# Sparse attention and two feed-forward stages: chunks of 4, 3, 5 and 4 blocks, and decoding tied behind the activations on VectorE

## The chip, the cores and the metric

The program runs on one core of a Trainium2 chip. The metric is the device time of one execution in microseconds (us). The engines are TensorE (PE, with its weight loads PEld), VectorE (DVE), ScalarE (ACT), GpSimd (POOL) and SyncE (SP, which starts the DMAs here). "L414" is line 414 of the kernel before; the changed kernel has one line more from line 473 on and three more at its end, so L486, L489 and L511 of before are L487, L490 and L512 after it.

## What is computed

```python
x = attention(q, k, v)              # 2 x 8 heads x 768 x 64: a window of +-15 keys and 24 block summaries
h = x @ w_in                        # 1536 x 512 by 512 x 2048
x = (h - np.tanh(h)) @ w_out        # 2048 x 512
rms = np.sqrt(np.mean(x * x, axis=-1, keepdims=True) + 1e-06)
xn = x / rms * rms_g
g = xn @ w_gate                     # 512 x 1536
silu = g * (1.0 / (1.0 + np.exp(-g)))
out = (silu * (xn @ w_val)) @ w_out2
```

The weights are 64-bit floats, which the kernel turns into pairs of 32-bit values on the chip.

## The kernel before

**Decoding.** A weight block of 512 x 128 (or 128 x 512) comes as 128 x 1024 32-bit words by one DMA (`load`). `words` makes 32-bit floats of it: ACT scales one half (L162), and three DVE operations put sign, exponent and mantissa together (L163, L164, L165). `split` makes a high part (ACT, L170) and a low part (POOL, L173), since every product is three matmuls: high by high, low by high, high by low (L395 to L397, L401 to L403). The decoding of one block is a Python generator, `one`, cut into portions at its `yield`s; for the second feed-forward `pair_of` also forms sums of quarters on POOL (L207 to L218), as Strassen's scheme with seven products needs them. `work()` emits the next portion; `adv(dt)` moves a planned clock on and emits a portion each `DEC` microseconds of it. A block needs a slot of ten (later thirteen) buffers, which is free again when the last group of tokens has used it.

**First feed-forward.** The 1536 tokens are four groups of 384, the 2048 inner columns sixteen blocks of 128, in chunks (`NCH`). The loops run over chunk, group, block; one pass of the inner body is a **step**, 64 in all. `up_step` does twelve matmuls into one of two PSUM banks `h`, then the activation: ACT's tanh (L413), DVE's difference (L414, which frees the bank), ACT's high part (L416), DVE's low part (L417). `down_step`, three steps later (`LAG`), does nine matmuls into three accumulators `acc`; at the last block of a chunk DVE adds these to `part` (L437; for the first chunk a copy, L435). Twelve steps lie among the attention, the other 52 behind it.

**Between the two.** After a group's last step, `norm` takes the mean square on ACT (L447), twelve small DVE operations that form the inverse root (L448 to L454), and a diagonal matrix from ACT (L457). `turn` transposes and scales `part` with matmuls (L474), ACT copies them out (L476), and `operand` forms the operands (DVE L486, ACT L488, DVE L489). `prepare` puts them on the planned clock.

**Second feed-forward.** Twelve units (six column blocks, two halves of the tokens) of fourteen products each (`unit2`, `product`); the activated pairs end with DVE's L511. Twelve down products (`down2`) of the unit before are filled in. The value weights' second half is read first by the unit's product "6" into `accx`.

**Order.** Tile, the layer underneath, takes the instructions with their dependences in the order of the Python text and lays each engine's order out by a simulated timeline. Each engine then works strictly in that order. `SLOTS_A`, `DEC`, the planned times and the text's order are the means of steering. `tc.issue_after(ins)` puts the instructions of its block that run on `ins`'s engine behind `ins` in that engine's order, without a semaphore.

Of the kernel before, what the change touches and what calls it, by code (L numbers as in the profile page):

```python
# [25 lines left out]
KT = TPB // 2  # L26
LOC = 64 + 2 * WIN
WID = LOC + NB
NCH = [4, 4, 4, 4]
NG = NT // GW  # L30
NP = FF2 // 256
SLOTS_A = 10
# [16 lines left out]
DTR = 6  # L49
DPV = 10  # L50
DVL = 10
DEC = (2.3, 1.9)
TP0 = 1.2
TP1 = 1.0
TC = 0.6
# [32 lines left out]
def attn_moe_kernel(ctx: ExitStack, tc: tile.TileContext, ins, out, dbg=None):  # L88
# [24 lines left out]
    def f(ap):  # L113
        return ap.bitcast(F32)
# [272 lines left out]
    for j, nch in enumerate(NCH):  # L387
# [1 line left out]
            for m in range(m0, m0 + nch):  # L389
                steps.append((j, g, m, m == m0, m == m0 + nch - 1))  # L390
        m0 += nch
    acc, part, gs = {}, {}, {}

    def triple(o, wh, wl, xh, xl, start, stop, **kw):
        T.matmul(o, wh, xh, start=start, stop=False, **kw)  # L395
        T.matmul(o, wl, xh, start=False, stop=False, **kw)  # L396
        T.matmul(o, wh, xl, start=False, stop=stop, **kw)  # L397

    def down(o, w, g, j, first, last):
        js = slice(j * 128, (j + 1) * 128)  # L400
        T.matmul(o, g[:, 0, js], w[:, 0], start=first, stop=False)  # L401
        T.matmul(o, g[:, 1, js], w[:, 0], start=False, stop=False)  # L402
        T.matmul(o, g[:, 0, js], w[:, 1], start=False, stop=last)  # L403

    def up_step(i):
        _, g, m, _, _ = steps[i]
        h = ps_h.tile([128, 512], F32, name="h")[:, 0:GW]
        w, x = wt["w_in", m], xT[g]
        for kk in range(KD):
            ws = slice(kk * 128, (kk + 1) * 128)  # L410
            triple(h, w[:, 0, ws], w[:, 1, ws], x[:, :, 0, kk], x[:, :, 1, kk], kk == 0, kk == KD - 1)
        t = tmp()
        A.activation(t, h, AF.Tanh)  # L413
        V.tensor_tensor(t, h, t, ALU.subtract)  # L414
        gg = gs[i] = gp.tile([128, 2, GW], F32R, name="g")
        A.activation(gg[:, 0], t, AF.Copy)  # L416
        V.tensor_tensor(gg[:, 1], t, f(gg[:, 0]), ALU.subtract)  # L417

    def down_step(i):
        j, g, m, first, last = steps[i]  # L420
        gg = gs.pop(i)
        for t in range(g * GT, g * GT + GT):
            if first:
                acc[t] = ps_a.tile([128, 512], F32, name="acc")
            down(acc[t], wt["w_out", m], gg, t - g * GT, first, last)
            if last:
                evac(acc.pop(t), t, j == 0)

    def evac(a, t, first):
# [40 lines left out]
    def turn(tp, kk, kh, half):  # L470
        g, k4 = 2 * tp + half, 2 * kh + kk
        ps = state["ps_t"].tile([128, 512], F32, name="t2")
        for j in range(GT):
            T.matmul(ps[:, j * 128:(j + 1) * 128], part[g * GT + j][:, k4 * 128:(k4 + 1) * 128], dg[g][:, j * 128:(j + 1) * 128], start=True, stop=True)  # L474
        xs[tp, kk, kh, half] = tmp()
        A.activation(xs[tp, kk, kh, half], ps[:, 0:GW], AF.Copy, scale=rg[:, k4:k4 + 1])  # L476
        adv(0.33)
# [23 lines left out]
    def unit2(p, tp, fill):  # L501
# [5 lines left out]
        def pair(s, row, half):  # L507
            g[row, half] = gp.tile([128, 2, GW], F32R, name="g")
            hi, lo = g[row, half][:, 0], g[row, half][:, 1]
            A.activation(hi, s, AF.Copy)  # L510
            V.tensor_tensor(lo, s, f(hi), ALU.subtract)  # L511

        product(ga, wg, tp, 1, True)
        s11 = tmp()
# [113 lines left out]
    n0 = NCH[0] * (NG - 1)  # L628
    at = TM0
    for i in range(n0):  # L630
        _, g, m, first, last = steps[i]
        req = [f"pv{g * GT + GT - 1}", f"w{m}"]
        if i >= LAG:
            req.append(f"dn{i - LAG}")
        task(f"up{i}", at, lambda i=i: up_step(i), *req)
        at += DM0
        task(f"dn{i}", at + LAG * DM0, lambda i=i: down_step(i), f"up{i}", f"w{NCH[0] + m}")
# [11 lines left out]
    def work():  # L649
        if free["gen"] is None:  # L650
            if nxt["job"] >= len(jobs):
                return False
            free["gen"] = decode(*jobs[nxt["job"]])
            nxt["job"] += 1
        r = next(free["gen"], 0)
        if r == 0:
            free["gen"] = None
        return r != "blocked"

    def adv(dt):  # L660
        free["t"] += dt
        if inside:
            return
        inside.append(1)
        while later and later[0][0] <= free["t"]:
            heapq.heappop(later)[2]()
        while free["at"] <= free["t"]:
            free["at"] = free["at"] + DEC[1 if prev else 0] if work() else free["t"] + 0.1
        inside.pop()

    def need(*keys):
# [5 lines left out]
    def prepare(tp, half, t, dt):  # L677
        if half == 0:
            operand_tiles(tp)
        for kk in range(2):  # L680
            for kh in range(2):
                at(t, lambda kk=kk, kh=kh: turn(tp, kk, kh, half))
                t += 0.5
            for n in (5, 6, 7, 4, 3) if half else (1, 2):
                at(t, lambda kk=kk, n=n: operand(tp, kk, n))
                t += dt
# [3 lines left out]
    for i in range(n0, len(steps) + LAG):  # L690
        if i < len(steps):
# [14 lines left out]
            if steps[i][1] == NG - 1 and ("w_in", steps[i][2]) not in LENT:  # L706
                free["n"] += 1
            adv(2.1)
        j, g, m, first, last = steps[i - LAG]
        need(("w_out", m))  # L710
        down_step(i - LAG)
        if g == NG - 1 and ("w_out", m) not in LENT:
            free["n"] += 1
        adv(2.1)
        if j == len(NCH) - 1 and last:
            t = free["t"]
            norm(g)
            prepare(g // 2, g % 2, t + 6.5, (1.0, 1.3, 1.0, 1.1)[g])

    for p in range(NP):  # L720
        need(("w_gate", p))
# [94 lines left out]
```

## Time and profile before

| | us |
|---|---|
| median of 3 runs | 673.13 (672.78 to 675.08) |
| profiled execution | 676.15 |
| its span, first to last instruction | 674.4 |
| PE busy in the span | 628.4 (93%) |
| DVE, ACT, POOL busy | 467.2, 324.4, 234.8 |

The span falls into attention with the first twelve steps (0 to about 125), the other 52 steps (to about 386), and the second feed-forward. The profiled execution lies 3.0 us above the median. A wait is put down to the engine whose semaphore came last; busy time of PE is modelled at its ends.

### The profile page before, as it was taken

The page shows a single profiled execution, that of the slowest core. Times are in us where ns is not written, and L with a number is a line of the kernel's source. Part 1 is how long each engine was busy: PE and PEld are TensorE (multiplying, and loading weights), DVE is VectorE, ACT ScalarE, POOL GpSimd, SP SyncE. Part 2 cuts the span into 40 slices and gives each one's busy share as a digit, 9 for nine tenths or more (in the row PEclk, how much of TensorE's full clock was granted, in tenths as well). Part 3 has the DMA queues.
Part 4 walks back from the last instruction along what each step waited for, and adds up shares of the span by engine and source line. Part 5 has one row for each costly group of instructions (what it writes and reads, how often), then busy time and mean ns, then how long its engine had stood idle before and what let it go on. Part 6 is the DMA issues. An engine that isn't in the chain of part 4 may idle for free.

```text
span 674.4 us, 9837 instructions
## 1 busy us (share of the span) xinstructions
PE 628.4 (93%) x3576; PEld 568.0 (84%) x3576; DVE 467.2 (69%) x979; ACT 324.4 (48%) x783; POOL 234.8 (35%) x237
## 2 busy tenths in 40 slices
PE   3769999989889879999999879999999999999997
PEld 3669898878777769999999779989999999999995
DVE  5899655499999873334448768777958968765545
ACT  2865676555455342223457666445444345353230
POOL 1568612034344730003003123527645556372100
PEclk9888999999999989999999989999999999999999
DMA  9995421144443330000000200211301402100013
GB/s 329 342 288 182 144 81 48 64 156 142 139 156 130 125 110 12 1 0 32 1 0 33 64 0 32 95 62 41 132 16 63 126 1 93 64 1 0 1 57 130
DMA packets 19641, 58.92 MB, mean 87 GB/s; under 512 B 2168, under 2 KB 5496, under 8 KB 19592
## 3 DMA queue, kind: packets, MB, share of 16 engines
q1 hardware_dynamic: 19592, 58.29, 25.7%
q8 instruction: 28, 0.46, 0.3%
q14 instruction: 21, 0.17, 0.1%
HBM read 54.84 MB, written 3.15 MB: 86 GB/s over the span
## 4 chain that ended last, share of the span: by engine, by line
PE 52%; DVE 15%; DMA 7%; issue 3%; ACT 3%; POOL 1%; DVEq 0%; SPq 0%; ACTq 0%
PE t L401 4%; PE h L395 4%; PE t L402 4%; PE t L403 4%; PE h L397 4%; PE h L396 4%; PE acc L395 4%; PE acc L396 4%; PE acc L397 3%; DVE dt L164 3%; DVE dt L165 3%; PE acc L403 3%; PE acc L402 3%; DMA raw<-w_out 3%; PE acc L401 3%
## 5 line engine op out<-in xcount | busy, mean ns | idle before, releaser
L173 POOL TENSOR_TENSOR w<-dt,w 128x512 fp32r<-128x512 f32 (+1 forms) x59 | 76.7, 1303 | 123.4 <-ACT w L170 109.0
L395 PE MATMUL h<-x,w 128*128 128x384 f32 x264 | 91.4, 346 | 6.2 <-DVE s L414 5.2
L397 PE MATMUL h<-x,w 128*128 128x384 f32 x264 | 89.8, 342 | 3.8 <-DVE x L382 3.8
L396 PE MATMUL h<-x,w 128*128 128x384 f32 x264 | 89.6, 339 | 0.0
L162 ACT ACTIVATE da<-raw 128x512 f32<-128x512 f32 x68 | 45.6, 671 | 88.3 <-DMA raw<-w_out 38.0
L173 POOL TENSOR_TENSOR w<-sf,w 128x256 fp32r<-128x256 f32 (+1 forms) x36 | 39.5, 1101 | 103.0 <-ACT w L170 101.7
L414 DVE TENSOR_TENSOR s<-h,s 128x384 f32<-128x384 f32 x64 | 35.3, 552 | 53.5 <-ACT s L413 53.5
L165 DVE SCALAR_TENSOR_TENSOR dt<-raw,dt 128x512 uint32<-128x512 uint32 x68 | 63.1, 930 | 0.7
L437 DVE TENSOR_TENSOR part<-t,part 128x512 f32<-128x512 f32 x60 | 40.3, 685 | 30.3 <-PE t L403 30.3
L395 PEld LDWEIGHTS h<-x,w 128*128 128x128 f32 x264 | 50.0, 190 | 12.1 <-DVE s L414 8.4
L164 DVE SCALAR_TENSOR_TENSOR dt<-da,dt 128x512 uint32<-128x512 uint32 x68 | 57.8, 852 | 3.2 <-ACT da L162 1.3
L402 PE MATMUL t<-w,g 128*128 128x512 f32 x144 | 56.9, 395 | 0.6 <-DVE g L511 0.6
L395 PE MATMUL acc<-x,w 128*128 128x384 f32 x168 | 56.9, 339 | 0.2 <-DVE part L437 0.2
L163 DVE TENSOR_SCALAR dt<-raw 128x512 uint32<-128x512 uint32 x68 | 42.7, 629 | 20.4 <-POOL w L173 6.1
L403 PE MATMUL t<-w,g 128*128 128x512 f32 x144 | 56.7, 394 | 0.0
L396 PE MATMUL acc<-x,w 128*128 128x384 f32 x168 | 56.5, 336 | 0.0
L397 PE MATMUL acc<-x,w 128*128 128x384 f32 x168 | 56.4, 337 | 0.0
L401 PE MATMUL t<-w,g 128*128 128x512 f32 x144 | 54.9, 394 | 0.3 <-DVE part L437 0.3
L397 PEld LDWEIGHTS h<-x,w 128*128 128x128 f32 x264 | 50.1, 190 | 5.1 <-DVE x L382 4.3
L413 ACT ACTIVATE s<-h 128x384 f32<-128x384 f32 x64 | 30.9, 483 | 48.8 <-PE h L397 48.6
L401 PE MATMUL acc<-w,g 128*128 128x512 f32 x132 | 51.0, 400 | 3.4 <-DVE part L437 3.2
L402 PE MATMUL acc<-w,g 128*128 128x512 f32 x132 | 52.1, 394 | 0.0
(130 smaller groups left out, 1548.5 us busy)
## 6 DMA issues: line engine op xcount, KB each, us to landing
raw<-w_out SPq DMA_DIRECT2D x28, 512.0 KB, 3.3
raw<-w_in SPq DMA_DIRECT2D x16, 512.0 KB, 3.7
q<-q SPq DMA_DIRECT2D x12, 512.0 KB, 7.8
raw<-w_gate SPq DMA_DIRECT2D x12, 512.0 KB, 3.4
raw<-w_val SPq DMA_DIRECT2D x12, 512.0 KB, 3.4
kw<-kw SPq DMA_DIRECT2D x8, 576.0 KB, 6.9
v<-vw SPq DMA_DIRECT2D x12, 384.0 KB, 5.3
out_dram<-part SPq DMA_DIRECT2D x12, 256.0 KB, 2.0
```

The source lines that it names most:

```text
L162: A.activation(a, r[:, :, 1].bitcast(F32), AF.Copy, scale=2.0 ** -112)
L163: V.tensor_scalar(t, r[:, :, 0], 29, None, ALU.logical_shift_right)
L164: V.scalar_tensor_tensor(t, a.bitcast(U32), 3, t, ALU.logical_shift_left, ALU.bitwise_or)
L165: V.scalar_tensor_tensor(t, r[:, :, 1], 0x80000000, t, ALU.bitwise_and, ALU.bitwise_or)
L173: G.tensor_tensor(lo, d, f(hi), ALU.subtract)
L395: T.matmul(o, wh, xh, start=start, stop=False, **kw)
L396: T.matmul(o, wl, xh, start=False, stop=False, **kw)
L397: T.matmul(o, wh, xl, start=False, stop=stop, **kw)
L401: T.matmul(o, g[:, 0, js], w[:, 0], start=first, stop=False)
L402: T.matmul(o, g[:, 1, js], w[:, 0], start=False, stop=False)
L403: T.matmul(o, g[:, 0, js], w[:, 1], start=False, stop=last)
L437: V.tensor_tensor(part[t], a, part[t], ALU.add)
```

## The change

The chunks become 4, 3, 5 and 4 blocks. Portions that `adv` emits are put, on DVE, behind the last low part traced so far (L417 or L511), and the turning products, on PE, behind the last product traced so far. The planned distance of portions in the first feed-forward is 1.8 in place of 2.3, and a group's turning is planned 9 in place of 6.5 behind its last step. `need` still emits portions without a tie.

```diff
-NCH = [4, 4, 4, 4]
+NCH = [4, 3, 5, 4]
-DEC = (2.3, 1.9)
+DEC = (1.8, 1.9)
...
-        T.matmul(o, wh, xl, start=False, stop=stop, **kw)
+        last["PE"] = T.matmul(o, wh, xl, start=False, stop=stop, **kw)
...
-        T.matmul(o, g[:, 0, js], w[:, 1], start=False, stop=last)
+        last["PE"] = T.matmul(o, g[:, 0, js], w[:, 1], start=False, stop=end)
...
-        V.tensor_tensor(gg[:, 1], t, f(gg[:, 0]), ALU.subtract)
+        last["DVE"] = V.tensor_tensor(gg[:, 1], t, f(gg[:, 0]), ALU.subtract)
...
-        for j in range(GT):
-            T.matmul(ps[:, j * 128:(j + 1) * 128], part[g * GT + j][:, k4 * 128:(k4 + 1) * 128], dg[g][:, j * 128:(j + 1) * 128], start=True, stop=True)
+        with tc.issue_after(last["PE"].ins):
+            for j in range(GT):
+                T.matmul(ps[:, j * 128:(j + 1) * 128], part[g * GT + j][:, k4 * 128:(k4 + 1) * 128], dg[g][:, j * 128:(j + 1) * 128], start=True, stop=True)
...
-            V.tensor_tensor(lo, s, f(hi), ALU.subtract)
+            last["DVE"] = V.tensor_tensor(lo, s, f(hi), ALU.subtract)
...
-            free["at"] = free["at"] + DEC[1 if prev else 0] if work() else free["t"] + 0.1
+            with tc.issue_after(last["DVE"].ins):
+                done = work()
+            free["at"] = free["at"] + DEC[1 if prev else 0] if done else free["t"] + 0.1
...
-            prepare(g // 2, g % 2, t + 6.5, (1.0, 1.3, 1.0, 1.1)[g])
+            prepare(g // 2, g % 2, t + 9, (1.0, 1.3, 1.0, 1.1)[g])
```

The order up to the last attention steps is the same. DVE's order differs from its 343rd row on, and PE's from its 349th.

**DVE, from the L414 of one step to the next, in the second chunk.** Before, from step 17 to step 18:

```order
L414 TENSOR_TENSOR s<-h,s 128x384
L165 SCALAR_TENSOR_TENSOR dt<-raw,dt 128x512
L163 TENSOR_SCALAR dt<-raw 128x512
L417 TENSOR_TENSOR g<-s,g 128x384
L164 SCALAR_TENSOR_TENSOR dt<-da,dt 128x512
L435 COPY part_1858<-acc 128x512
L165 SCALAR_TENSOR_TENSOR dt<-raw,dt 128x512
L163 TENSOR_SCALAR dt<-raw 128x512
L164 SCALAR_TENSOR_TENSOR dt<-da,dt 128x512
L435 COPY part_1868<-acc 128x512
L165 SCALAR_TENSOR_TENSOR dt<-raw,dt 128x512
L414 TENSOR_TENSOR s<-h,s 128x384
```

After the change, from step 22 by way of step 23 to step 24:

```order
L414 TENSOR_TENSOR s<-h,s 128x384
L165 SCALAR_TENSOR_TENSOR dt<-raw,dt 128x512
L417 TENSOR_TENSOR g<-s,g 128x384
L163 TENSOR_SCALAR dt<-raw 128x512
L164 SCALAR_TENSOR_TENSOR dt<-da,dt 128x512
L165 SCALAR_TENSOR_TENSOR dt<-raw,dt 128x512
L414 TENSOR_TENSOR s<-h,s 128x384
L417 TENSOR_TENSOR g<-s,g 128x384
L163 TENSOR_SCALAR dt<-raw 128x512
L164 SCALAR_TENSOR_TENSOR dt<-da,dt 128x512
L165 SCALAR_TENSOR_TENSOR dt<-raw,dt 128x512
L414 TENSOR_TENSOR s<-h,s 128x384
```

Before, two whole decodings and the end of a third lie between one step's L414 and the next, parts of them between L414 and L417; after the change one does at most, behind that step's L417. In the whole order before, the 31 decodings from the ninth to the 39th stand between the L414s of steps 11 and 36, and the next behind step 50's. After the change the 28 from the ninth to the 36th stand between the L414s of steps 12 and 48, with 23 of the operations L435 and L437 among them.

**PE, end of the first feed-forward.** `g_3583` and `g_3666` are the activations of steps 62 and 63, `part2_1712` (`part2_1715` after the change) belongs to the third group, `h_3839` is a product of the second feed-forward in the bank that step 63's L414 frees. Before, the end of step 62's down product and the third group's first turning:

```order
L403 MATMUL acc_3692<-x2_2789,g_3583 128x512
L474 MATMUL t2_3719<-s_3649,part2_1712 128x128
L474 MATMUL t2_3725<-s_3649,part2_1712 128x128
L474 MATMUL t2_3719<-s_3649,part2_1717 128x128
L474 MATMUL t2_3725<-s_3649,part2_1717 128x128
L474 MATMUL t2_3719<-s_3649,part2_1722 128x128
L474 MATMUL t2_3725<-s_3649,part2_1722 128x128
L395 MATMUL h_3839<-x2_3220,w_3263 128x384
L396 MATMUL h_3839<-x2_3220,w_3263 128x384
L397 MATMUL h_3839<-x2_3220,w_3263 128x384
L395 MATMUL h_3839<-x2_3220,w_3263 128x384
L396 MATMUL h_3839<-x2_3220,w_3263 128x384
```

After the change, from the last matmul of the same product into `h_3839`, over step 63's down product:

```order
L397 MATMUL h_3839<-x2_3260,w_3054 128x384
L401 MATMUL acc_3682<-w_2783,g_3666 128x512
L401 MATMUL acc_3686<-w_2783,g_3666 128x512
L401 MATMUL acc_3690<-w_2783,g_3666 128x512
L402 MATMUL acc_3682<-w_2783,g_3666 128x512
L403 MATMUL acc_3682<-w_2783,g_3666 128x512
L402 MATMUL acc_3686<-w_2783,g_3666 128x512
L403 MATMUL acc_3686<-w_2783,g_3666 128x512
L402 MATMUL acc_3690<-w_2783,g_3666 128x512
L403 MATMUL acc_3690<-w_2783,g_3666 128x512
L475 MATMUL t2_3732<-s_3643,part2_1715 128x128
L475 MATMUL t2_3732<-s_3643,part2_1720 128x128
```

The third group's turnings have moved from ahead of step 63's down product to behind it, and the second half of the second group's from ahead of step 59's down product to behind it.

**DVE, second feed-forward.** `dt_4592` is the second half of the third value block. Before, it begins behind the sixth of the 48 L511s:

```order
L511 TENSOR_TENSOR g_4145<-s_4063,g_4145 128x384
L435 COPY part_4035<-t2_4028 128x512
L557 TENSOR_TENSOR s_4124<-accx_4040,s_4124 128x384
L163 TENSOR_SCALAR dt_4592<-raw_4517 128x512
L511 TENSOR_TENSOR g_4161<-s_4124,g_4161 128x384
L164 SCALAR_TENSOR_TENSOR dt_4592<-da_4591,dt_4592 128x512
L163 TENSOR_SCALAR dt_4704<-raw_4685 128x512
L511 TENSOR_TENSOR g_4172<-s_4071,g_4172 128x384
L165 SCALAR_TENSOR_TENSOR dt_4592<-raw_4517,dt_4592 128x512
```

After the change it begins behind the fourteenth (L512 there):

```order
L512 TENSOR_TENSOR g_4580<-s_4450,g_4580 128x384
L163 TENSOR_SCALAR dt_4592<-raw_4517 128x512
L518 TENSOR_TENSOR s_4646<-acc_4637,s_4646 128x384
L562 TENSOR_TENSOR s_4458<-s_4458,s_4535 128x384
L164 SCALAR_TENSOR_TENSOR dt_4592<-da_4591,dt_4592 128x512
L437 TENSOR_TENSOR part_4035<-t2_4597,part_4035 128x512
L165 SCALAR_TENSOR_TENSOR dt_4592<-raw_4517,dt_4592 128x512
L558 TENSOR_TENSOR s_4543<-accx_4417,s_4543 128x384
L512 TENSOR_TENSOR g_4619<-s_4543,g_4619 128x384
```

The decoding has moved back by eight activated pairs, and three operations of the unit lie among its own three.

## Rows read from the trace of the kernel before

**Rows 1.** Page, part 1: busy time, share of the span, instructions of TensorE.
```profile
PE 628.4 (93%) x3576; PEld 568.0 (84%) x3576; DVE 467.2 (69%) x979; ACT 324.4 (48%) x783; POOL 234.8 (35%) x237
```

**Rows 2.** Stretches: us, busy of PE, PEld, DVE, ACT, POOL, clock, DMA share, GB/s.
```profile
125.00:250.00 125.00, 110.57 (x579) 95.22 (x579) 110.59 (x160) 61.79 (x119) 50.18 (x41) 0.99 0.40 135
275.00:300.00 25.00, 25.00 (x128) 22.74 (x127) 10.10 (x18) 6.11 (x12) 0.00 (x0) 1.00 0.00 1
375.00:400.00 25.00, 19.56 (x106) 17.41 (x105) 14.75 (x42) 16.50 (x38) 5.36 (x7) 0.93 0.07 22
475.00:500.00 25.00, 25.00 (x131) 23.17 (x130) 18.28 (x30) 10.20 (x22) 9.99 (x9) 1.00 0.20 70
```

**Rows 3.** PE's waits from 125 to 250: total us, times, longest.
```profile
PE h L395 <- DVE s L414: 9.4, 9, 2.2
PE acc L401 <- DVE part L437: 3.2, 4, 2.2
PE h L397 <- DVE x L382: 1.5, 1, 1.5
```

**Rows 4.** DVE's groups from 131.3 to 234.7: busy us, mean ns | idle before.
```profile
L165 DVE SCALAR_TENSOR_TENSOR dt<-raw,dt 128x512 uint32<-128x512 uint32 x28 | 28.3, 1010 | 0.3
L164 DVE SCALAR_TENSOR_TENSOR dt<-da,dt 128x512 uint32<-128x512 uint32 x28 | 25.3, 905 | 1.9 <-ACT da L162 1.0
L163 DVE TENSOR_SCALAR dt<-raw 128x512 uint32<-128x512 uint32 x28 | 16.5, 589 | 6.3 <-issue 3.5 <-DMA raw<-w_in 2.0 <-DMA raw<-w_val 0.6
L417 DVE TENSOR_TENSOR g<-s,g 128x384 fp32r<-128x384 f32 x20 | 14.5, 725 | 0.0
```

**Rows 5.** Timeline of DVE, two quiet steps: start us, us, instruction [idle before <-releaser].
```profile
272.61 0.56 DVE L414 TENSOR_TENSOR s<-h,s 128x384 f32<-128x384 f32 x1 [2.50 <-ACT s L413]
273.75 0.56 DVE L417 TENSOR_TENSOR g<-s,g 128x384 fp32r<-128x384 f32 x1 [0.59 <-ACT g L416]
276.81 0.56 DVE L414 TENSOR_TENSOR s<-h,s 128x384 f32<-128x384 f32 x1 [2.49 <-ACT s L413]
277.28 1.28 DVE L437 TENSOR_TENSOR part<-acc,part 128x512 f32<-128x512 f32 x2
```

**Rows 6.** Timeline of DVE, one decoding with no other work beside it.
```profile
131.39 0.43 DVE L163 TENSOR_SCALAR dt<-raw 128x512 uint32<-128x512 uint32 x1 [3.48 <-issue]
132.09 0.69 DVE L164 SCALAR_TENSOR_TENSOR dt<-da,dt 128x512 uint32<-128x512 uint32 x1 [0.28 <-ACT da L162]
132.82 0.69 DVE L165 SCALAR_TENSOR_TENSOR dt<-raw,dt 128x512 uint32<-128x512 uint32 x1
```

**Rows 7.** Stretches of 5 us after two of PE's gaps, columns as in group 2.
```profile
245.00:250.00 5.00, 4.94 (x17) 4.57 (x18) 5.00 (x10) 2.04 (x5) 1.87 (x2) 0.66 0.29 105
390.00:395.00 5.00, 1.89 (x9) 1.89 (x10) 2.87 (x11) 2.74 (x7) 1.10 (x2) 0.76 0.00 0
```

**Rows 8.** Timeline of PE where the first feed-forward ends: turning products.
```profile
379.74 1.60 PE L474 MATMUL t<-s,part 128*128 128x128 f32 x12 [1.77 <-ACT s L457]
...
393.11 2.93 PE L474 MATMUL t<-s,part 128*128 128x128 f32 x12 [3.46 <-ACT s L457]
```

**Rows 9.** Timeline of DVE: first and last of the third group's twelve norm operations.
```profile
374.38 0.15 DVE L448 TENSOR_SCALAR rv<-rv 128x3 f32<-128x3 f32 x1
...
379.09 0.16 DVE L454 SCALAR_TENSOR_TENSOR ry<-rt,ry 128x3 f32<-128x3 f32 x1
```

**Rows 10.** Second feed-forward: one timeline row of DVE, one of PE, three of POOL.
```profile
481.01 0.54 DVE L511 TENSOR_TENSOR g<-s,g 128x384 fp32r<-128x384 f32 x1
...
491.37 0.34 PE L395 MATMUL accx<-x,w 128*128 128x384 f32 x1
...
502.78 1.28 POOL L173 TENSOR_TENSOR w<-dt,w 128x512 fp32r<-128x512 f32 x1
504.02 0.74 POOL L207 TENSOR_TENSOR sf<-dt 128x256 f32<-128x256 f32 x1
...
506.56 0.93 POOL L218 TENSOR_TENSOR sf<-dt,sf 128x256 f32<-128x256 f32 x1
```

More of the change, by code (lines that the diff above doesn't have):

```diff
@@ L391, in attn_moe_kernel @@
         m0 += nch
-    acc, part, gs = {}, {}, {}
+    acc, part, gs, last = {}, {}, {}, {}
     def triple(o, wh, wl, xh, xl, start, stop, **kw):
@@ L396, in triple, with down @@
         T.matmul(o, wl, xh, start=False, stop=False, **kw)
-        T.matmul(o, wh, xl, start=False, stop=stop, **kw)
-    def down(o, w, g, j, first, last):
+        last["PE"] = T.matmul(o, wh, xl, start=False, stop=stop, **kw)
+    def down(o, w, g, j, first, end):
         js = slice(j * 128, (j + 1) * 128)
@@ L416, in up_step @@
         A.activation(gg[:, 0], t, AF.Copy)
-        V.tensor_tensor(gg[:, 1], t, f(gg[:, 0]), ALU.subtract)
+        last["DVE"] = V.tensor_tensor(gg[:, 1], t, f(gg[:, 0]), ALU.subtract)
     def down_step(i):
-        j, g, m, first, last = steps[i]
+        j, g, m, first, end = steps[i]
         gg = gs.pop(i)
@@ L424, in down_step @@
                 acc[t] = ps_a.tile([128, 512], F32, name="acc")
-            down(acc[t], wt["w_out", m], gg, t - g * GT, first, last)
-            if last:
+            down(acc[t], wt["w_out", m], gg, t - g * GT, first, end)
+            if end:
                 evac(acc.pop(t), t, j == 0)
@@ L630, in attn_moe_kernel @@
     for i in range(n0):
-        _, g, m, first, last = steps[i]
+        _, g, m, _, _ = steps[i]
         req = [f"pv{g * GT + GT - 1}", f"w{m}"]
@@ L708, in attn_moe_kernel @@
             adv(2.1)
-        j, g, m, first, last = steps[i - LAG]
+        j, g, m, first, end = steps[i - LAG]
         need(("w_out", m))
@@ L714, in attn_moe_kernel @@
         adv(2.1)
-        if j == len(NCH) - 1 and last:
+        if j == len(NCH) - 1 and end:
             t = free["t"]
             norm(g)
-            prepare(g // 2, g % 2, t + 6.5, (1.0, 1.3, 1.0, 1.1)[g])
+            prepare(g // 2, g % 2, t + 9, (1.0, 1.3, 1.0, 1.1)[g])
     for p in range(NP):
```

## The prediction

> **What bounds the kernel now.** The page comes first: PE is busy for 628.4 of 674.4 us [rows 1], so all that an order can give back is 46 us. Then the stretches of 25 us, for where these lie [rows 2]. The reader is to see four kinds of stretch. From 275 to 300 and from 475 to 500 PE has no gap, although DVE works there for 10.10 or 18.28 of 25 us: those stretches are bound by PE, and nothing in them is to be had. From 125 to 250, where steps 12 to 35 run, PE is busy for 110.57 of 125 us (14.4 idle) while DVE is busy for 110.59. From 375 to 400, where the first feed-forward hands over to the second, PE is idle for 5.4 us. The rest lies in the attention, whose order the change leaves alone, and in the last evictions.
>
> The third view is the list of PE's waits in the second kind [rows 3]: 9.4 us for L414, which frees the bank `h`, 3.2 for the addition L437 that frees an accumulator, 1.5 for L382. All are DVE's, together 14.1 of the 14.4. None of these operations is long; they stand behind decodings in DVE's order. DVE is not too slow for the stage as a whole: in the quiet steps L414 comes every 4.20 us (272.61 to 276.81) and DVE then waits 2.49 us for the next [rows 5]. It is asked for 31 decodings in 24 steps and then for none in the next 15.
>
> **Part 1, the decodings (all of chunks, distance and tie).** No instruction is added, and PE's count of matmuls stays; a wait goes. After the change 28 decodings stand over 36 steps. What DVE needs there: a step without decoding takes from 272.61 to 274.31, 1.70 us, the gap of 0.59 in it included [rows 5]: 36 x 1.70 = 61.2. A decoding is (28.3 + 25.3 + 16.5) / 28 = 2.50 us in the dense stretch [rows 4], and 0.43 + 0.69 + 0.69 = 1.81 alone [rows 6]. Additions at 0.64 (half of 1.28 [rows 5]): 23 x 0.64 = 14.7. The upper sum is 61.2 + 28 x 2.50 + 14.7 = 146, the lower 61.2 + 28 x 1.81 + 14.7 = 127. PE needs 36 x 4.20 = 151. Both sums fit, the upper one with 3% to spare; and they are high, since neighbours overlap (276.81 to 277.28 is 0.47 for an operation of 0.56 [rows 5]).
>
> The 0.69 us between the two prices is a block by POOL: L165 takes 1010 ns on average against 690 alone, and L417 takes 725 against 560 [rows 4 to 6]. The Trainium skill (SBUF — State Buffer, "Who interferes with whom") says that a DVE operation with two SBUF inputs and a GpSimd operation that reads SBUF exclude each other for a whole instruction, whichever starts first. By that rule the block speaks against the change, as an L417 with its activation waiting can be the loser wherever a subtraction of a decoding now falls, so that the upper sum, 146, holds; if the block went where DVE idles, the lower, 127, would. The rows show L417 longer, so the trace agrees.
>
> A single step can still exceed PE's: decoding and three additions are 1.70 + 2.50 + 1.92 = 6.1 us, 1.9 over. That is covered: with two banks, L414 may be late by about a step (4.20) before PE stops, and a down product comes three steps after its activation. If the cover is gone, each further us is PE's. So of 14.4 us of gaps I take 3.0 as left, a fifth, for crowded steps; the ends are 0 (both sums fit) and 7 (half). Gain **11.4** (7.4 to 14.4).
>
> With the gaps goes a slow clock: from 245 to 250 PE had 0.66 of its clock, after a gap [rows 7]; that is 2.4 GHz for part and 1.2 GHz for the rest, and costs 0.34 x 5 = **1.7** us. I count it whole; the ends are 0 (a left gap brings it back) and 1.7.
>
> What comes late next: the weights. The ninth block (`w_in` 4) is now decoded behind step 13's L417 and no longer before step 12. PE reads it in step 16, three steps or 12.6 us after step 13; a decoding needs 2.50, POOL's subtraction 1.28 [rows 10], and ACT's copy between them is taken as 1.28 too: 5.1 in all. Later blocks have more: in the order every block stands two or more steps before its use. Cost 0, cover over 7 us. SP's loads come as raw buffers free up, so they spread likewise. The 1.5 us for L382 go too: no decoding stands ahead of it now.
>
> **Part 2, the turning.** At the hand-over PE waits twice for L457: 1.77 us for the third group's, 3.46 for the fourth's [rows 8]. The change moves 12 turning products of the third group behind step 63's down product, and 6 of the second group behind step 59's. (The rows show 12 passes for 6 products.) The first wait doesn't vanish: a product into the bank that step 63's L414 frees stands there now, and on ACT that step's L413 stands behind the same L457. But the two turnings between this wait and step 63's down product (1.60 each, 3.2 us) now fall into the second wait, and 1.6 us of second-group turning into the first. Taken alone, that shortens the stretch by up to 3.6 us: 1.6 at the first wait, and 3.2 less 1.2 at the second, as L413 and L414 (0.6 each, 0.56 in [rows 5]) now follow L457 before PE goes on. Against it, DVE's twelve norm operations, which took 4.9 us for the third group (374.38 to 379.25) because operand operations lie among them [rows 9], get two more of 0.55 there and two for the fourth group, 2.2 us. Net **1.4**; the ends are -3 (both chains longer by three times that) and 3.6. The clock there (0.76 from 390 to 395 [rows 7]) stays as it is, since a gap remains.
>
> The Trainium skill (TensorE: Matmul & The Clock Gate, "What's actually happening") says that the slow clock is the default and activity lifts it. By that rule the 1.7 us of part 1 come back only if the gaps before 245 do, and the loss at 390 stays; the two stretches in the rows, each slow after a gap, agree.
>
> **Part 3, the second feed-forward.** The same tie holds there. The value blocks' second halves move back by eight pairs, to the end of the unit before the one that reads them. In the trace, from the end of such an L511 (481.55) to the first read of the last-made half in the next unit (491.37) are 9.8 us [rows 10]. The way through is three operations of 0.55, a decoding of 1.81 to 2.50, POOL's four sums in 3.5 (504.02 to 507.49) and three subtractions of 1.28 at most [rows 10]: 10.8 to 11.5. That would be late by 1.0 to 1.7 us in each of five blocks, 5 to 8.5. But before, that L511 itself stood behind early decodings of 2 to 3 us, which are gone from its front, so it comes sooner. I take **-1.0**, nearer to the cover, with 0 and -8.5 for ends.
>
> **Sum.** 11.4 + 1.7 + 1.4 - 1.0 = 13.5 us. The profiled execution took 676.15, so it would be 662.6; the median of the runs lies 3.0 lower, and gives 673.13 - 13.5 = **659.6 us**.
>
> **Rivals.**
> 1. *DVE stays the bound.* For it: the upper sum is 97% of PE's, and an operation that waits in DVE's order can't be passed any more by a decoding. Against it: both sums fit. If gaps of 9 remain and the clock stays slow, the gain is 5.4 + 1.4 - 1.0 = 5.8: about 667.
> 2. *The hand-over closes as well.* For it: the turnings move to where PE waits. Against it: L457 still ends both waits. The 5.2 us of its gaps less the 1.4 already counted, and a clock of 1.2 (0.24 x 5), would come on top: about 655.
> 3. *Weights late instead.* The first chunk border moves the wait from L414 to the ninth to eleventh block; for it: nothing is decoded ahead of step 12 any more. Against it: 12.6 us of lead. If each border (three) gave back 4 us, the time would be 672, within 0.5%.
> 4. *Slower: the value weights.* The way of part 3 decides from 9.8 us on. If DVE's three operations wait for PE too, and POOL's order sets the next unit's product ahead of the last subtraction, it takes some 14 us: 4 or more late, five times, and a slow clock after each (0.34 x 5): 5 x 5.7 = 28, so 659.6 + 28 - 1 = about 687. Against it: PE's order after the change reads that half no earlier.
>
> The change cannot fail to do what it says: the order shows the ties in place.
>
> **Numbers.** A measurement of this kernel can tell about 0.5% from no change. Chances: forecast 0.60 (its own range 654 to 666, from the ends of parts 1 and 2), rival 1 0.16, rival 2 0.08, rival 3 0.09, rival 4 0.07. Faster by over 0.5% (below 669.8) are the forecast and rivals 1 and 2: 0.84; within: 0.09; slower: 0.07. Leaving out the two last rivals and little else, the range is 652 to 669.
>
> **What would show it.** Right: between 125 and 250 PE's gaps are 3 us or so, its waits for L414 near 2 in place of 9.4, DVE's busy time there below 100, more of it from 250 to 310; the stretch from 245 on has a clock of 1.00. The two waits for L457, or for L414 ahead of it, still sum to 4 to 6 us. After 400 PE has no gap. Wrong: waits of PE for L170 or L173 in the first feed-forward (rival 3), waits for DVE of over 7 us there (rival 1), or a gap of 1 us or more in every second unit at the first read of the value weights (rival 4).

## The result, and the profile after

| | before | after |
|---|---|---|
| median, us (4 runs each) | 674.11 (672.78 to 679.88) | 657.64 (656.81 to 658.37) |
| profiled execution, us | 676.15 | 658.16 |
| its span, us | 674.4 | 656.4 |

The ratio is 0.9739, 95% interval 0.968 to 0.9799: faster by 16.5 us. Forecast were 13.5 us and 659.6. That the sum came out so near is in part luck: the first of its three parts gave more than forecast, and the second lost where a gain was forecast. The stages show it.

The page of the kernel after, busy times (before: [rows 1]):

```profile
PE 625.1 (95%) x3576; PEld 571.3 (87%) x3576; DVE 451.1 (69%) x979; ACT 324.6 (49%) x783; POOL 227.7 (35%) x237
```

PE's idle time fell from 46.0 to 31.3 us. Stretches of the kernel after, columns as in [rows 2]:

```profile
125.00:250.00 125.00, 125.00 (x665) 112.87 (x660) 91.22 (x149) 58.00 (x109) 28.97 (x22) 1.00 0.29 100
245.00:250.00 5.00, 5.00 (x27) 4.60 (x27) 4.75 (x8) 2.10 (x4) 2.00 (x2) 1.00 0.44 168
350.00:375.00 25.00, 18.36 (x90) 15.99 (x88) 18.65 (x48) 11.64 (x29) 6.97 (x7) 0.86 0.11 40
375.00:400.00 25.00, 23.32 (x129) 22.85 (x130) 17.40 (x34) 19.02 (x42) 4.01 (x3) 0.93 0.00 1
400.00:640.00 240.00, 240.00 (x1250) 223.63 (x1249) 165.56 (x268) 108.27 (x230) 109.75 (x111) 1.00 0.17 59
```

From 125 to 250 PE has no gap at all, where it had 14.4 us, and the clock at 245 is back at its upper level (0.66 in [rows 7]). DVE's busy time there fell from 110.59 to 91.22. From 400 on PE is full. But the hand-over now has two gaps that sum to 8.3 us, against 5.2 in [rows 8], and more slow clock. PE's waits from 250 to 400 in the kernel after (total us, times, longest):

```profile
PE h L395 <- DVE s L414: 6.4, 1, 6.4
PE t L475 <- ACT s L477: 2.0, 1, 2.0
```

For a balance by stages I take two marks that stand in both traces: L414 of step 11 and L414 of step 54. Timeline of DVE before, then after:

```profile
125.56 0.56 DVE L414 TENSOR_TENSOR s<-h,s 128x384 f32<-128x384 f32 x1 [2.74 <-ACT s L413]
...
327.09 0.56 DVE L414 TENSOR_TENSOR s<-h,s 128x384 f32<-128x384 f32 x1 [2.48 <-ACT s L413]
```

```profile
124.89 0.56 DVE L414 TENSOR_TENSOR s<-h,s 128x384 f32<-128x384 f32 x1 [2.74 <-ACT s L413]
...
306.47 0.56 DVE L414 TENSOR_TENSOR s<-h,s 128x384 f32<-128x384 f32 x1 [2.62 <-ACT s L413]
```

These 43 steps took 201.5 us and take 181.6: **19.9 gained**. From step 54 to the end it was 347.3 and is 349.9: **2.6 lost**. The 0.7 gained ahead of step 11 is not the change's: up to there the traces show the same operations in the same order, and the kernels below, for which that holds too, reach the mark anywhere between 125.3 and 127.0. The sum, 18.0, is the difference of the spans.

The gaps of [rows 3] (14.4) and the slow clock (1.7) make only 16.1 of the 19.9. The rest is in what a gap hides. Timeline of PE before, around one wait:

```profile
193.91 0.39 PE L402 MATMUL acc<-w,g 128*128 128x512 f32 x1
194.13 0.39 PE L403 MATMUL acc<-w,g 128*128 128x512 f32 x1
195.46 0.44 PE L395 MATMUL h<-x,w 128*128 128x384 f32 x1 [0.94 <-DVE s L414]
195.75 0.34 PE L396 MATMUL h<-x,w 128*128 128x384 f32 x1
195.92 0.34 PE L397 MATMUL h<-x,w 128*128 128x384 f32 x1
```

Unbroken, the second of these starts 0.22 after the first, so L395 could have started at 194.35; it started 1.11 later, while the row's idle time says 0.94. It then holds its successor up for 0.29 where 0.17 is usual. So this gap cost some 1.2 us, 0.27 over its idle time. Worked out from the starts in the same way, each of the 15 gaps from 125 to 250 (the 14 of [rows 3] and one of 0.2 us) costs 0.24 to 0.27 more than its idle time, 3.9 us in all, and 14.4 + 1.7 + 3.9 = 20.0.

### The profile page after: what moved, and what is told of

Its sections match the earlier page's. It is cut to its first block, busy times and chain, and to the rows that moved or that the text cites. A ratio compares the mean times of both kernels' runs of the same rounds, so it can differ in the third digit from the quotient of the medians.

```text
span 656.4 us, 9788 instructions
## 1 busy us (share of the span) xinstructions
PE 625.1 (95%) x3576; PEld 571.3 (87%) x3576; DVE 451.1 (69%) x979; ACT 324.6 (49%) x783; POOL 227.7 (35%) x237
## 4 chain that ended last, share of the span: by engine, by line
PE 86%; DVE 9%; ACT 2%; issue 1%; DMA 1%; POOL 0%; SPq 0%; DVEq 0%; ACTq 0%
PE h L395 8%; PE h L397 8%; PE h L396 8%; PE acc L401 6%; PE acc L402 6%; PE acc L403 6%; PE t L401 5%; PE t L402 5%; PE t L403 5%; PE acc L395 4%; PE acc L397 4%; PE acc L396 4%; PE accx L397 3%; PE accx L396 3%; PE accx L395 3%; PE t L346 2%
## 5 line engine op out<-in xcount | busy, mean ns | idle before, releaser
L173 POOL TENSOR_TENSOR w<-dt,w 128x512 fp32r<-128x512 f32 (+1 forms) x59 | 73.8, 1252 | 191.6 <-ACT w L170 139.8
L395 PE MATMUL h<-x,w 128*128 128x384 f32 x248 | 85.5, 345 | 7.5 <-DVE s L414 6.4
L397 PE MATMUL h<-x,w 128*128 128x384 f32 x248 | 84.7, 343 | 2.3 <-DVE x L382 2.3
L396 PE MATMUL h<-x,w 128*128 128x384 f32 x248 | 84.6, 341 | 0.0
L414 DVE TENSOR_TENSOR s<-h,s 128x384 f32<-128x384 f32 x64 | 35.5, 555 | 46.5 <-ACT s L413 46.2
L417 DVE TENSOR_TENSOR g<-s,g 128x384 fp32r<-128x384 f32 x64 | 47.5, 743 | 22.4 <-ACT g L416 22.2
L395 PE MATMUL acc<-x,w 128*128 128x384 f32 x168 | 57.8, 344 | 0.0
L402 PE MATMUL acc<-w,g 128*128 128x512 f32 x144 | 57.2, 397 | 0.0
L437 DVE TENSOR_TENSOR part<-t,part 128x512 f32<-128x512 f32 x60 | 40.5, 686 | 23.2 <-PE t L403 23.2
L395 PEld LDWEIGHTS h<-x,w 128*128 128x128 f32 x248 | 47.3, 191 | 10.5 <-DVE s L414 6.8
L403 PE MATMUL acc<-w,g 128*128 128x512 f32 x144 | 56.1, 397 | 0.0
L401 PE MATMUL acc<-w,g 128*128 128x512 f32 x144 | 55.3, 400 | 0.0
L164 DVE SCALAR_TENSOR_TENSOR dt<-da,dt 128x512 uint32<-128x512 uint32 x68 | 53.8, 791 | 1.6
L165 DVE SCALAR_TENSOR_TENSOR dt<-raw,dt 128x512 uint32<-128x512 uint32 x68 | 51.4, 756 | 1.3
L170 ACT ACTIVATE w<-dt 128x512 fp32r<-128x512 f32 (+1 forms) x55 | 32.0, 583 | 40.7 <-DVE dt L165 40.2
L413 ACT ACTIVATE s<-h 128x384 f32<-128x384 f32 x64 | 30.9, 483 | 41.2 <-PE h L397 41.0
```

What stands on the lines that cost most here:

```text
L164: V.scalar_tensor_tensor(t, a.bitcast(U32), 3, t, ALU.logical_shift_left, ALU.bitwise_or)
L165: V.scalar_tensor_tensor(t, r[:, :, 1], 0x80000000, t, ALU.bitwise_and, ALU.bitwise_or)
L173: G.tensor_tensor(lo, d, f(hi), ALU.subtract)
L397: last["PE"] = T.matmul(o, wh, xl, start=False, stop=stop, **kw)
L403: last["PE"] = T.matmul(o, g[:, 0, js], w[:, 1], start=False, stop=end)
L417: last["DVE"] = V.tensor_tensor(gg[:, 1], t, f(gg[:, 0]), ALU.subtract)
```

## The experiments

The kernels were timed in five sets, each with runs of the kernel before beside it: the kernel after; e1 to e4; e5 to e8; e9 to e11; e12. The median of the kernel before lay between 674.1 and 677.1 us in them, so medians of different sets are compared to 2 us at best, and the stages decide. "To 54" is the time from step 11's L414 to step 54's, "from 54" from there to the end, "gaps" PE's idle time from 340 to 400 us, and "chain" the third group's norm in DVE's timeline, from the start of L448 to the end of the last L454; these four are from the profiled execution.

| kernel | median (all runs) | ratio to before, 95% | to 54 | from 54 | gaps | chain |
|---|---|---|---|---|---|---|
| before | 674.1 to 677.1 | 1 | 201.5 | 347.3 | 5.4 | 4.87 |
| after | 657.64 (656.81-658.37) | 0.9739 (0.968-0.9799) | 181.6 | 349.9 | 8.3 | 6.52 |
| e1 no tie | 676.74 (674.74-678.55) | 1.0009 (0.9987-1.0031) | 196.4 | 351.8 | 9.0 | 5.63 |
| e2 equal chunks | 659.99 (659.2-660.89) | 0.9754 (0.9723-0.9784) | 182.6 | 348.1 | 8.1 | 6.52 |
| e3 turning as before | 658.84 (655.87-659.28) | 0.9727 (0.9691-0.9762) | 181.8 | 346.2 | 6.4 | 7.98 |
| e4 tie alone | 667.38 (666.93-667.66) | 0.9862 (0.9832-0.9891) | 184.8 | 353.8 | 11.6 | 9.14 |
| e5 distance 2.3 | 661.0 (660.75-662.29) | 0.978 (0.9743-0.9818) | 181.4 | 351.3 | 10.5 | 10.34 |
| e6 tie in the first only | 664.94 (663.63-666.03) | 0.9832 (0.9798-0.9865) | 181.7 | 354.6 | 10.7 | 6.52 |
| e7 norm later | 654.49 (652.58-654.7) | 0.9672 (0.9639-0.9705) | 181.7 | 344.7 | 4.7 | 10.17 |
| e8 norm later, turning as before | 652.91 (651.83-653.13) | 0.9651 (0.962-0.9683) | 181.8 | 343.4 | 3.7 | 9.98 |
| e9 tie in the second only | 668.67 (666.2-670.47) | 0.9878 (0.9842-0.9914) | 195.1 | 344.9 | 4.9 | 4.62 |
| e10 equal chunks, 2.3 | 665.54 (665.05-665.93) | 0.9832 (0.9806-0.9858) | 184.7 | 353.1 | 11.6 | 10.96 |
| e11 norms together | 654.16 (652.89-655.01) | 0.9665 (0.9641-0.9689) | 181.9 | 344.3 | 5.3 | 9.98 |
| e12 tie behind the norms | 649.92 (649.03-650.71) | 0.9615 (0.959-0.9641) | 181.6 | 340.1 | 2.1 | 7.94 |

### Is it the tie, the distance, or the chunks? (e1, e2)

```diff
-            with tc.issue_after(last["DVE"].ins):
-                done = work()
+            done = work()
```

> The changed kernel with the tie on DVE taken out; chunks of 4, 3, 5, 4, the distance 1.8 and the turning stay. In DVE's order four decodings then stand ahead of step 12's L417 again and up to two ahead of each of the next twenty, as in the kernel before. Theory (the tie carries the gain): from 125 to 250 us TensorE idles for 11 to 16 us again, waits for L414 sum to 7 us or more, the clock dips below 1.00 there, and the time is 669 to 676. Rival (chunks and distance carry it): TensorE idles for 3 us at most there and the time is 655 to 661.

Without the tie the whole gain is gone: 676.74, ratio 1.0009. PE's stretch and its first waits there:

```profile
125.00:250.00 125.00, 114.66 (x605) 100.19 (x604) 107.37 (x159) 61.46 (x118) 48.59 (x38) 0.99 0.40 131
```

```profile
PE h L395 <- DVE s L414: 7.8, 6, 3.1
PE acc L401 <- DVE part L437: 1.2, 1, 1.2
```

10.3 us of gaps (I had said 11 at least, and 676 at most for the time), L414 again in front. Chunks, distance and turning alone save 5.1 us up to step 54 and lose 4.5 behind it, at the hand-over. So nothing is gained without the tie.

```diff
-NCH = [4, 3, 5, 4]
+NCH = [4, 4, 4, 4]
```

> The changed kernel with chunks of 4, 4, 4, 4; both ties, the distance and the turning's time stay. DVE's decodings stand ahead of the same steps. Theory (the tie carries the gain): no gap from 125 to 250 us, and the time within 2 us of the changed kernel's 657.6. Rival (the chunks keep accumulators and weights in time): L437 or late weights cost 3 us or more between 125 and 250, and the time is over 661.

The median is 2.3 above the changed kernel's, a bit more than the theory allowed and less than the rival asked; no gap from 125 to 250, and the two ratios' intervals overlap. In the profiled executions the time from step 11's mark on is 0.8 us less. At this distance no effect of the chunks can be told.

### The tie's two halves (e6, e9)

```diff
-            with tc.issue_after(last["DVE"].ins):
+            with (contextlib.nullcontext() if prev else tc.issue_after(last["DVE"].ins)):
```

(e9: the two branches exchanged.)

> The changed kernel with the tie on DVE in the first feed-forward alone; in the second the decodings are free again as in the kernel before. Theory (the second feed-forward is bound by TensorE either way): at most 1.5 us of gaps from 400 us on, and the time within 1.5 us of 657.6. Rival (the tie costs there, as part 3 of the prediction has it, or without it decodings stand ahead of the unit's own operations): the time is lower or higher by over 2 us, with gaps after 400 us to show for it.

> The changed kernel with the tie on DVE in the second feed-forward alone; in the first the decodings are free. Theory (two separate gains: the first feed-forward's part of the tie closes 10 us of gaps from 125 to 250 us and lifts the clock there, the second's keeps three decodings out of the hand-over): gaps of 9 to 13 us from 125 to 250, gaps of 7 to 9 us from 340 to 400, none after 400, and a time of 667 to 672. Rival (the second's part is worth nothing once the first's is gone): 674 to 678, as without any tie.

The theory of e6 fell: 664.94, 7.3 us more. That of e9 held in its time, 668.67, and in the gaps from 125 to 250 (10.8); at the hand-over they are 4.9 where I had 7 at least. With e1 and the changed kernel they make a square: the first half is worth 676.74 - 664.94 = 11.8 or 668.67 - 657.64 = 11.0 us, the second 7.3 or 8.1. Within the 2 us that medians of different sets allow, they add up. By the stages the first half gains 14.7 us up to step 54 (e1 to e6) or 13.5 (e9 to the kernel after) and gives 2.8 or 5.0 of it back behind that mark; the second gains 4.7 (e6 to the kernel after) or 6.9 (e1 to e9) there. The second does not act where part 3 of the prediction looked. In e6 PE has 1.1 us of gaps from 400 to 640, none of them at the value weights; most is lost before 400:

```profile
340.00:400.00 60.00, 49.30 (x267) 46.04 (x267) 49.14 (x98) 37.60 (x86) 18.75 (x18) 0.91 0.13 45
```

The same stretch of the kernel after:

```profile
340.00:400.00 60.00, 51.67 (x282) 48.45 (x281) 45.29 (x97) 38.87 (x89) 13.47 (x12) 0.91 0.08 27
```

In e6 DVE is busy for 3.9 us more and POOL for 5.3 more: untied, three decodings stand between step 63's L417 and the second feed-forward's first L511 in DVE's order, where one stands when tied. They run in the hand-over, and the wait at the fourth group's turning is 4.3 in place of 2.0 (in e6 every line number is one higher):

```profile
PE t L476 <- ACT s L478: 4.3, 1, 4.3
```

Between e1 and e9 it is other decodings: none stands behind step 63's L417 in either, but in e1 two begin at 361.21 and 366.92, ahead of the third group's norm, and in e9 none begins from 358 to 400.

### The distance, and what chunks do at the old one (e4, e5, e10)

```diff
 e4, on the kernel before:
...
+            with tc.issue_after(last["DVE"].ins):
...
 e5, on the kernel after:
-DEC = (1.8, 1.9)
+DEC = (2.3, 1.9)
 e10, on e5:
-NCH = [4, 3, 5, 4]
+NCH = [4, 4, 4, 4]
```

> The kernel before with the tie on DVE alone; chunks of 4 blocks, distance 2.3, turning as before. Theory (the tie carries the gain): from 125 to 250 us TensorE idles for 2 us at most, and the time is 652 to 658. Rival (it needs the new distance and chunks): at the distance of 2.3 decodings come too late, TensorE waits for weights for 5 us or more in all, and the time is 662 to 670.

> The changed kernel with the distance between portions at 2.3 in place of 1.8; chunks of 4, 3, 5, 4, both ties and the turning's time stay. In DVE's order decodings then reach into steps 51 to 63, nine of them in the last fourteen steps, where the changed kernel has four. Theory (the tie needs the shorter distance, so that the hand-over's norm chains meet no decodings): no more than 3 us of gaps from 125 to 250 us, but gaps of 10 to 14 us from 340 to 400, and a time of 663 to 668. Rival (what the tie alone lacked against the changed kernel came from its chunks or its turning): the time is 656 to 661.

> The changed kernel with chunks of 4, 4, 4, 4 and the distance 2.3; both ties and the turning's time stay. It stands between the tie alone (667.4, turning as before) and the changed kernel at distance 2.3 (661.0, chunks of 4, 3, 5, 4). Theory (at the distance 2.3 the turning without a tie waits for a norm chain that decodings stretch, which the tied turning hides in part): gaps of 8.5 to 11 us from 340 to 400 us, and a time of 660 to 664. Rival (at that distance the equal chunks bring the weights late): PE's wait for L170 of 1.6 us and some 2.8 us of gaps from 125 to 250 come back, and the time is 665 to 669.

Neither text on e4 had it all: the gaps from 125 to 250 are 2.8, not the 2 or 5, and the time, 667.38, is the rival's, but most is lost elsewhere. Up to step 54 the tie alone saves 16.7 us of the 19.9. PE's waits in e4, first from 125 to 250, then from 250 to 400:

```profile
PE h L395 <- ACT w L170: 1.6, 1, 1.6
PE h L395 <- DVE s L414: 1.2, 1, 1.2
```

```profile
PE t L475 <- ACT s L457: 11.6, 2, 7.3
```

e5 splits it: with chunks of 4, 3, 5, 4 the distance 2.3 costs nothing up to step 54 (181.4), and 2.2 us of gaps at the hand-over, where the chain is 10.34 us. These gaps, 10.5, are the theory's, but the time, 661.0, is at the rival's upper end and not 663 or more: the distance is worth 3.4 us by the medians and 1.2 by the stages. e10 was a miss of mine: the rival held. With equal chunks the wait of 1.6 us for L170 comes back at the same place as in e4, with 665.54. So the 4, 3, 5, 4 matters at the old distance (to 54: 184.7 against 181.4), while at the new one no effect of it can be told (182.6 against 181.6): up to step 54 either of the two is enough. Between e4 and e10 the turning makes 1.8 us by the medians, which are of two sets, and 0.7 from step 54 on.

### The turning, and the third norm's place (e3, e7, e8)

```diff
-        with tc.issue_after(last["PE"].ins):
+        if True:
...
-            prepare(g // 2, g % 2, t + 9, (1.0, 1.3, 1.0, 1.1)[g])
+            prepare(g // 2, g % 2, t + 6.5, (1.0, 1.3, 1.0, 1.1)[g])
```

> The changed kernel with the turning as before (no tie on TensorE, 6.5 in place of 9). Theory (the moved turning costs the hand-over: its two gaps were 5.2 us before and are 8.4 now, with more slow clock): the gaps sum to 4 to 6 us again and the time falls by 3 to 5 us, to 653 to 655. Rival (the hand-over is longer because decodings and operands that the tie on DVE holds back fall on the norm chain): the gaps stay at 7 us or more and the time within 1.5 us of 657.6.

Unclear. The gaps fell to 6.4 and the profiled execution took 655.87, but the three others took 658.8 to 659.3, so that the median is 658.84 where the theory wanted 655 at most. That the moved turning costs 3 us or more is not borne out; that it gains anything isn't either.

The chain of waits at the hand-over of the kernel after is plain in its timelines. DVE:

```profile
350.95 1.10 DVE L417 TENSOR_TENSOR g<-s,g 128x384 fp32r<-128x384 f32 x1
351.97 1.09 DVE L490 TENSOR_TENSOR x<-s,x 128x384 fp32r<-128x384 f32 x1
352.98 1.09 DVE L487 TENSOR_TENSOR s<-s 128x384 f32<-128x384 f32 x1
354.00 1.09 DVE L490 TENSOR_TENSOR x<-s,x 128x384 fp32r<-128x384 f32 x1
355.00 1.25 DVE L448 TENSOR_SCALAR rv<-rv 128x3 f32<-128x3 f32 x1
...
361.36 0.16 DVE L454 SCALAR_TENSOR_TENSOR ry<-rt,ry 128x3 f32<-128x3 f32 x1
362.95 0.56 DVE L414 TENSOR_TENSOR s<-h,s 128x384 f32<-128x384 f32 x1 [1.42 <-ACT s L413]
```

ACT:

```profile
361.56 0.99 ACT L457 ACTIVATE s<-sel,ry 128x128 f32<-128x128 f32 x3 [1.68 <-DVE ry L454]
362.45 0.46 ACT L413 ACTIVATE s<-h 128x384 f32<-128x384 f32 x1
```

PE:

```profile
363.56 0.69 PE L395 MATMUL h<-x,w 128*128 128x384 f32 x1 [6.38 <-DVE s L414]
```

Step 63's L413 had its product early and stands behind L457, which stands behind a norm of twelve tiny operations with eight L487 and L490 among them. So e7 moves that norm's issue behind step 63's up product:

```diff
-    prev = None
+    prev, due = None, []
...
+            if i == len(steps) - 1:
+                due.pop()()
...
-            norm(g)
+            if g == 2:
+                due.append(lambda: norm(2))
+            else:
+                norm(g)
```

> The changed kernel with the third group's norm issued behind step 63's up product, so that L413 and L416 of step 63 stand ahead of L457 in ScalarE's order. Theory (the 6.4 us wait is step 63's L414 behind L413 behind L457): the wait for L414 falls below 1 us, the wait at the fourth group's turning grows by 1 to 3 us, and the time is 652 to 655. Rival (the chain of the two norms sets the end of the hand-over whatever stands between): the fourth group's turning takes the whole of it up, the gaps still sum to 7 us or more and the time stays within 1.5 us of 657.6.

> The same with the turning as in the kernel before (no tie on TensorE, 6.5 in place of 9). Theory (the turning's place matters little by itself): within 1.5 us of the run with the norm later alone. Rival (an untied turning stands ahead of step 63's down product and waits for L457 again): a wait of 3 us or more for L457 ahead of that down product, and 2 us or more slower than the norm later alone.

e7: 654.49, 3.2 us less, as the theory had it; no wait for L414 is left. The new ones are not where I put them: 3.2 for L437, the eviction of step 63's accumulators, which stands behind the first six of the norm's operations in DVE's order, and 1.5 at the turnings, which is less than the 2.0 of the kernel after and not 1 to 3 more. e8, with the turning as before on top, is 1.6 us better still (theory: within 1.5), and has no wait of 3 us ahead of step 63's down product. So in this place the moved turning is worth between nothing and a loss of 1.6 us.

### Two tries at the rest (e11, e12)

```diff
 e11: norm(2) and its turning behind step 63's down product, right ahead of norm(3), the turning untied
 e12, on e8:
-            V.scalar_tensor_tensor(y, r, 1.5, y, ALU.add, ALU.mult)
+            last["DVE"] = V.scalar_tensor_tensor(y, r, 1.5, y, ALU.add, ALU.mult)
```

> The changed kernel with the third group's norm and turning issued behind step 63's down product, right ahead of the fourth's, the turning untied on TensorE. Theory (what is left of the wait is the eviction of step 63's accumulators, which stands behind the third norm's chain in DVE's order): the wait for L437 of 2.3 us goes, the gaps from 340 to 400 us sum to 3 us or less, and the time is 650 to 652. Rival (both norm chains, one behind the other, end later than the products that cover them): waits of 4 us or more for L457 or L477, and a time of 654 or more.

> The run with the norm later and the turning as before, and the tie on DVE extended: a norm's last operation L454 also counts as the operation behind which the next portion of a decoding stands. In DVE's order the decoding that lay among the third norm's twelve operations (0.96, 1.78 and 0.68 us there, with the eviction of step 63's accumulators behind it) then stands behind the fourth norm. Theory (decodings among the norm's operations and POOL's work make the rest of the hand-over): the third norm's chain falls from 9.98 to 6 to 7 us, the wait for L437 of 2.3 us falls below 1, the gaps from 340 to 400 us sum to 2.5 us or less, and the time is 649.5 to 651.5. Rival (operands and POOL alone stretch the chain): the chain stays at 9 us or more, the gaps at 3.5, and the time within 1 us of 652.9.

e11 missed, 654.16, which is the rival's time, though not by the rival's waits: the operations' issue was moved, but the scheduler still put the third norm, all but its last operation, ahead of L437 on DVE, with a chain of 9.98 as in e8, and the wait for L437 stayed:

```profile
PE acc L395 <- ACT s L516: 3.0, 1, 3.0
PE acc L395 <- DVE part L437: 2.3, 1, 2.3
```

e12 met its theory, 649.92, but for the chain, which is 7.94 and not 6 to 7. In e8 one decoding lay inside it:

```profile
355.92 0.96 DVE L163 TENSOR_SCALAR dt<-raw 128x512 uint32<-128x512 uint32 x1
...
358.90 1.78 DVE L164 SCALAR_TENSOR_TENSOR dt<-da,dt 128x512 uint32<-128x512 uint32 x1
...
361.14 0.68 DVE L165 SCALAR_TENSOR_TENSOR dt<-raw,dt 128x512 uint32<-128x512 uint32 x1
```

In e12 it begins behind the fourth norm. Only PE's two waits for L457 are left, and the clock stays at its upper level through the hand-over:

```profile
PE t L475 <- ACT s L457: 2.1, 2, 1.3
```

```profile
340.00:400.00 60.00, 57.87 (x329) 54.05 (x328) 50.06 (x105) 42.17 (x95) 14.44 (x13) 1.00 0.09 27
```

This kernel beats both: 0.9615 of before, and 7.7 us under the kernel after.

## Why the prediction was right, and where it was wrong

**Part 1** was right in its mechanism and too small: 13.1 forecast (11.4 and 1.7 of clock), 19.9 in the stage. Two terms failed. "I take 3.0 as left, a fifth, for crowded steps": none was left, the end 14.4 of the range. And a gap was priced at its idle time, which leaves out the 3.9 worked out above. The forecast's own range does not follow from the ends named for it either: 7.4 + 1.7 - 3 - 1.0 = 5.1 gives 668 and not 666. The clock's 1.7 came back whole. What the sums for DVE show is that both were high: in the kernel after DVE is busy for 91.22 us from 125 to 250, with 30 L417s, so 3.0 us a step, where they gave 3.5 and 4.1, with 0.59 of idle time counted in. DVE's groups there:

```profile
L417 DVE TENSOR_TENSOR g<-s,g 128x384 fp32r<-128x384 f32 x30 | 22.2, 739 | 10.9 <-ACT g L416 10.9
L164 DVE SCALAR_TENSOR_TENSOR dt<-da,dt 128x512 uint32<-128x512 uint32 x22 | 18.9, 859 | 0.6
...
L165 DVE SCALAR_TENSOR_TENSOR dt<-raw,dt 128x512 uint32<-128x512 uint32 x22 | 15.1, 688 | 0.4
...
L163 DVE TENSOR_SCALAR dt<-raw 128x512 uint32<-128x512 uint32 x22 | 9.2, 418 | 0.0
```

A decoding fell from 2.50 us [rows 4] to 0.86 + 0.69 + 0.42 = 1.97, close to the lone 1.81: POOL is busy for 28.97 us beside them, where it was for 50.18 [rows 2], and most of its block went with the crowd. L417 kept its share of the block, 739 ns against 725.

That the parts of the change were taken together in part 1 hid which of them carries it: the tie does. In that stage it saves 16.7 us alone (e4), and the rest of the change saves 5.1 without it (e1); distance and chunks keep the weights in time for it (e5, e10).

**Part 2** had the wrong sign: +1.4 forecast. From the end of step 59's down product to the fourth group's turning it took 25.1 us before (368.03 to 393.11) and takes 30.4 after (346.25 to 376.68); less the 1.25 of second-group turning that moved into it, that is 4.1 lost. Two steps failed. The first is "two more of 0.55 there and two for the fourth group, 2.2 us". From the start of the group's last L437 to L457 the third group's way grew by 3.7 us, from 8.0 (371.27 to 379.29) to 11.7 (349.88 to 361.56): eight operand operations lie in the chain in place of five and one of a decoding, and five rows ahead of and at its head took 1.09 to 1.25 us each, as POOL worked for a decoding beside them. The fourth group's norm took 3.03 us in place of 3.78 and did not grow. The second step is "the clock there stays as it is". Before, PE resumed behind the third group's wait at a granted clock of 1.00 and kept it up to the fourth's; now it resumes at 363.56 at 1.2 GHz and runs so for 4.33 us (columns as in [rows 2], the clock third from the end):

```profile
363.56:367.89 4.33, 4.33 (x12) 3.87 (x13) 2.28 (x4) 0.50 (x1) 0.00 (x0) 0.50 0.08 23
```

Half of that, 2.2 us, is an estimate of its cost; PE's idle time from 340 to 400 grew by 2.9 (5.4 to 8.3). Together they are 1.0 more than the 4.1, and where that came back stays open. In e12, with 2.1 us of idle time, the clock does not fall. The turnings were also taken at their rows' 1.60 us, where one takes 1.26 from its start to the next product's (364.63 to 365.89 before). The moved turning's share isn't settled: by the medians it lies between a gain of 1.2 us (e3) and a loss of 1.6 (e8 beside e7), but the profiled execution of e3, the fastest of its four, is 3.7 shorter behind step 54. What was missed is that the tie in the first feed-forward holds decodings of the next stage back into the hand-over (2.8 to 5.0 us behind step 54, e6 and e9), and that L413 of step 63, which the prediction named as standing behind L457, then waits for all of it (e7).

**Part 3** had the wrong sign too: -1.0 forecast. From the fourth group's turning to the end it took 281.3 us and takes 279.7; no gap stands at the value weights, so "late by 1.0 to 1.7 us in each of five blocks" did not come, and PE's gaps from 400 to 640, 1.1 us before, are gone. And the tie in the second feed-forward keeps decodings out of the hand-over, which the prediction does not have: 4.7 to 6.9 us behind step 54, 7.3 to 8.1 by the medians (e6, e9).

Rival 1 was refuted (no gap, not 9 us), rival 2 as well (the hand-over opened further), rival 3 at this distance (no wait for L170; at 2.3 with equal chunks it is real, 1.6 us, e10). Of the signs listed, the gaps, L414's waits, DVE under 100, the clock from 245 on and the full stretch after 400 came as told or better; "4 to 6 us" for the hand-over did not, at 8.3.

Open stays how the hand-over's loss divides between POOL's block and the operand operations: no run took POOL's work out of it alone. By the rows, some 2.7 of the 3.7 us are an estimate for the block: four at 1.09 where 0.55 is usual and L448 at 1.25 where [rows 9] has 0.15, 3.3 in all, less 0.5 for one L417 of 1.05 that met it before (371.87). And e3's four executions do not agree among themselves, so the turning's worth in the changed kernel itself is known only to some 2 us.

## What to carry to other kernels

Where an engine with time to spare makes another wait, look at what stands ahead of the awaited operation in its order; a tie of the work that can wait behind the work that can't was here worth the whole gap, once the distance between portions or the chunks kept the weights in time. Test such a tie by stages, since it moves work as well: what it held back here fell on the hand-over, and gave the next 7.7 us once the norms were put into the same order. When a gap is priced, add what the pipeline loses at its two ends.

## What was not expected of the hardware

A wait of PE cost 0.24 to 0.27 us more than the idle time its row shows, in each of the 15 gaps from 125 to 250 before. Part of it lies in the row before the gap, whose end is modelled: rows of 0.39 us follow each other at 0.22 when PE runs on. The other part lies behind the gap, where the next product starts 0.29 later in place of 0.17.

DVE and POOL took turns: from 350.95 to 356.2 DVE's rows above last 1.09 to 1.25 us, and POOL's beside them 1.05 to 1.60:

```profile
351.59 1.05 POOL L208 TENSOR_TENSOR sf<-sf,dt 128x256 f32<-128x256 f32 x1
352.60 1.05 POOL L173 TENSOR_TENSOR w<-sf,w 128x256 fp32r<-128x256 f32 x1
353.61 1.06 POOL L218 TENSOR_TENSOR sf<-dt,sf 128x256 f32<-128x256 f32 x1
354.63 1.60 POOL L173 TENSOR_TENSOR w<-sf,w 128x512 fp32r<-128x512 f32 x1
```

Each starts within 0.4 us ahead of a row of DVE's. Even L448, an operation with one input of 128x3, took 1.25 where it takes 0.17 when POOL rests (372.11 in the same kernel). The Trainium skill (SBUF — State Buffer, "Who interferes with whom") counts the tensor_scalar among the operations that can take the shared ports in a two-port mode, and says that the other engine is then blocked and not slowed; the trace agrees for L448. L414, one of whose inputs lies in PSUM, takes 555 ns on average from 125 to 250, no more than in the quiet steps of [rows 5].
